# Binding the two stores of an output buffer in order, in a list-scheduled attention and adapter kernel

## Chip, cores and metric

The kernel runs on one core of a Trainium2 chip. The metric is device time in microseconds (us). The kernel before takes 130.53 us (median of 3 runs, 130.23 to 131.1). "The profile" is the record of one execution: its engines are PE (matmul), PEld (weight load), DVE (vector), ACT (scalar), POOL (GpSimd) and SP, which here only issues DMAs. The span of a profile is about 1.8 us shorter than the time of its run. The profiled run of the kernel before took 131.71 us, 1.2 us above the median. A run is called slow when it is over 1.5% above the fastest of its kernel; ratios leave slow runs out.

## The reference

```
q_p, k_p = phi(q), phi(k)            # relu(x) times a cosine and a sine of the position
num = q_p @ (k_p^T v);  den = q_p . sum(k_p) + 1e-6
x   = (num / den), heads side by side          # 4608 rows of 512, float32
logits = x @ w_gate;  the two best of 8 experts, softmax weights w
out = x + sum over the two of  w * (x @ A[e]) @ B[e]
```

Eight batches of q, k and v (28.3 MB with the weights left out) are loaded and 9.4 MB are stored.

## The kernel before

The rows are worked on in 36 groups of 128. One or two groups make a *unit*, which is collected in one output buffer ("osb", a pool of seven). ACT evicts (copies out) the result of a group from PSUM, where PE leaves it, into the buffer (`x_sum`; one of the last is DVE's). Two DMA stores then empty the buffer: y=0 the lower 64 partitions, y=1 the upper 64.

```python
def x_sum(g, eng):                      # eviction of group g
    dx = st[g].pop("dx")
    u, j = unit_of[g]
    if u not in osbs:
        osbs[u] = p_out.tile([NP, 2, DM], FP32, name="osb")    # p_out has bufs=7
    copy(eng, osbs[u][:, j, :], dx)

def store(u, y, eng):                   # half y of unit u
    osb = osbs[u]
    ...
    {"SP": nc.sync, "ACT": nc.scalar, "POOL": nc.gpsimd}[eng].dma_start(
        out=dst[:, x:x + 2 * n - 1:2, :], in_=osb[SP * y:SP * y + SP, 0:n, :])
```

The order of all instructions is made when the kernel is built. Each piece of work is declared as an `op` with its engine, an estimated cost, a priority, what it depends on (`deps`), the buffers that it takes and those that it gives back. A list scheduler (`plan`) goes forward and backward through these declarations and returns an order; the instructions are then emitted in that order. The program itself does not trust the declarations: real semaphores are set from what each instruction truly reads and writes. A wrong declaration can therefore not give a wrong result. It can give a plan in which a real wait is missing.

```python
NB = {..., "osb": 7, ...}               # buffers that the plan counts
for g in range(G):
    ...                                 # cut
    op(("os", g), e, {"ACT": 0.5, "DVE": 0.6}[e], p + 1, lambda g=g, e=e: x_sum(g, e),
       deps=[("dx", g)], take=["osb"] if unit_of[g][1] == 0 else [], give=[bank])
    u, n = unit_of[g]
    if n == len(units[u]) - 1:
        for y in range(2):
            op(("st", u, y), "SP", 0.6, p + 2 + y, lambda u=u, y=y: store(u, y, "SP"),
               deps=[("os", h) for h in units[u]], take=["lane"], lat=1.3)
            op(("out", u, y), "DMA", 0.34 * (n + 1), p + 3 + y, none, deps=[("st", u, y)],
               give=["lane"] + (["osb"] if y else []), lat=0.4)

for n in plan(ops, NB):
    ops[n].fn()
```

("lane" is one of eight DMAs that the plan allows in flight.) The last `give` is the point: the plan hands the buffer back when the store y=1 has landed, and says nothing of y=0.

## Time and profile before

| | kernel before |
|---|---|
| time, median | 130.53 us |
| span of the profile | 129.9 us |
| busy PE / DVE / ACT / POOL | 87.7 / 89.3 / 90.4 / 82.7 us |
| longest wait of an eviction for a store | 11.2 us |
| DMA rate while it is full | about 395 GB/s |

The page of the kernel before cuts the span into 40 slices of 3.25 us; a digit is the busy tenth of a slice (9 is 90% or more), PEclk the granted PE clock in tenths of full speed.

```profile
PE   0007785599989879889978400099998999967400
DVE  0594687845999998899999300058899999984200
ACT  7755079877999978989999300295999656877500
POOL 4035975799999999999985994058999700000000
PEclk9999999856999999999999965557999999999955
DMA  4999999999999999999999999987350164752984
```

About three fifths of the way PE and DVE read 0 for three slices and ACT for two, while DMA stays full and POOL goes on a little longer. The PE clock falls to a half in the same place and recovers only later. The next view puts numbers to it: busy time by stretch (from:to in us, its length, then us busy and instructions of each engine, the granted clock as a share of full speed, DMA share and rate; the DMA share can read a little over 1).

```profile
core 0: us, PE busy (x) PEld busy (x) DVE busy (x) ACT busy (x) POOL busy (x), PEclk, DMA share, GB/s
31.00:72.60 41.60, 36.59 (x732) 29.27 (x741) 38.88 (x121) 38.87 (x96) 39.64 (x74) 0.99 1.05 395
72.60:83.80 11.20, 0.47 (x30) 0.44 (x23) 0.24 (x1) 0.05 (x2) 6.99 (x16) 0.65 1.05 397
83.80:91.80 8.00, 7.14 (x76) 5.65 (x77) 5.16 (x12) 6.41 (x16) 5.32 (x12) 0.64 0.78 219
```

Up to 72.6 us this is a balanced pipeline in which four engines are all over 87% busy. Then there is a hole of 11.2 us. The list of waits (who waited for whom: us in total, times, longest) names its cause:

```profile
PE dx L461 <- ACT osb L197: 12.3, 4, 11.4
DVE wg L430 <- ACT sg L423: 12.0, 2, 11.7
ACT osb L197 <- DMA out_dram<-osb: 11.2, 1, 11.2
...
POOL qp L206 <- PE qTp L335: 6.9, 2, 6.5
```

Read it from the third line. One eviction on ACT waited once, for 11.2 us, for a store. The other lines are followers: ACT executes in order, so PE waits for ACT's eviction, DVE for a sigmoid that stands behind it on ACT, and POOL for PE. The chain that ended last (start, us, what) passes through the same store:

```profile
69.19 0.55 SPq L191
69.74 0.05 issue
69.79 13.90 DMA out_dram<-osb
...
83.79 0.59 ACT osb L197
84.43 0.59 PE dx L461
```

The store that was waited for was put in the queue at 69.79 us, just after the last load (69.19), and landed 13.9 us later. The order in which SP issues DMAs explains why it came so late (place in the queue; buffer numbers kept):

```
20 store osb_703    21 load v    22 load k    23 store osb_703
24 store osb_855    25 store osb_1109     26 load k   27 load v
28 store osb_1227   29 load q    30 load q    31 store osb_1389
32 load k   33 load v   34 store osb_1446     35 load q   (the last load)
36 store osb_855    37 store osb_1109     38 store osb_1553     39 store osb_1227 ...
```

The buffer osb_855 has one half stored at place 24, the other at 36.

The store at place 36 was not slow for its stage, it was issued late. By the landing records of the trace every store that was put in the queue between 39 and 70 us (places 20 to 36) took 10 to 14 us to land. An estimate from the same records agrees: at 69.79 us four loads of 1.18 MB and two stores (0.13 and 0.26 MB) had not landed; with this store that is 5.4 MB, or 13.6 us at 395 GB/s. The other half, at place 24, was issued at 46.61 us and landed at 59.34.

### The profile page before, as it was taken

How to read it: one execution, taken by the hardware profiler on the slowest of the kernel's cores; microseconds unless marked ns; L12 is line 12 of the kernel's file. 1: busy time of each engine (PE TensorE's matmuls, PEld its weight loads, DVE VectorE, ACT ScalarE, POOL GpSimd, SP SyncE). 2: the span in 40 equal slices, each digit the busy share in tenths (PEclk: the TensorE clock that was granted, in tenths of full speed). 3: DMA queues.
4: the chain of work that ended last, by engine and by line, in shares of the span. 5: the costliest groups of instructions: out<-in, count | busy, mean ns of one | idle time of the engine just before them, and what ended most of it. 6: DMA issues, size and time to landing. Idle time of an engine off the chain costs nothing.

```text
span 129.9 us, 4085 instructions
## 1 busy us (share of the span) xinstructions
PE 87.7 (67%) x1580; PEld 69.4 (53%) x1596; DVE 89.3 (69%) x273; ACT 90.4 (70%) x214; POOL 82.7 (64%) x168
## 2 busy tenths in 40 slices
PE   0007785599989879889978400099998999967400
PEld 0007565488667667667757300077786788644100
DVE  0594687845999998899999300058899999984200
ACT  7755079877999978989999300295999656877500
POOL 4035975799999999999985994058999700000000
PEclk9999999856999999999999965557999999999955
DMA  4999999999999999999999999987350164752984
GB/s 120 367 371 358 383 390 395 397 392 382 393 393 387 392 389 402 392 399 405 397 397 395 400 390 405 386 239 194 87 138 32 37 166 124 176 146 87 241 217 107
DMA packets 19379, 38.55 MB, mean 297 GB/s; under 512 B 1696, under 2 KB 2720, under 8 KB 19360
## 3 DMA queue, kind: packets, MB, share of 16 engines
q1 hardware_dynamic: 19360, 38.29, 85.0%
q8 instruction: 12, 0.20, 0.6%
q14 instruction: 7, 0.06, 0.1%
HBM read 28.85 MB, written 9.44 MB: 295 GB/s over the span
## 4 chain that ended last, share of the span: by engine, by line
DVE 25%; DMA 21%; PE 20%; POOL 11%; SPq 8%; issue 5%; ACT 3%; ACTq 0%; POOLq 0%
DMA out_dram<-osb 11%; DMA vf<-in_v_dram 10%; DVE xt L367 9%; POOL qp L206 7%; PE qTp L335 6%; DVE qT L341 5%; SPq L191 4%; PE kvz L299 4%; POOL vb_118 L199 3%; DVE zg L432 3%; DVE xT L199 2%; SPq L486 2%; PE za L397 2%; POOL vb_120 L199 2%; DVE rden L365 2%
## 5 line engine op out<-in xcount | busy, mean ns | idle before, releaser
L206 POOL TENSOR_SCALAR qp<-qf,cos_tab 128x256 bf16<-128x256 f32 x71 | 33.9, 478 | 11.1 <-PE qTp L335 6.9
L204 ACT ACTIVATE kp<-kf,cos_tab 128x256 bf16<-128x256 f32 (+1 forms) x69 | 34.2, 495 | 6.1 <-DMA kf<-in_k_dram 6.1
L206 POOL TENSOR_SCALAR qp<-qf,sin_tab 128x256 bf16<-128x256 f32 x71 | 33.9, 477 | 0.0
L204 ACT ACTIVATE kp<-kf,sin_tab 128x256 bf16<-128x256 f32 (+1 forms) x69 | 33.8, 490 | 0.0
L197 ACT COPY osb<-dx 128x512 f32<-128x512 f32 x31 | 17.9, 579 | 16.5 <-DMA out_dram<-osb 11.2
L341 DVE TENSOR_SCALAR qT<-qTp 128x1024 bf16<-128x1024 bf16 x36 | 24.6, 684 | 5.9 <-PE qTp L335 5.9
L335 PE MATMUL qTp<-ident,qp 128*128 128x128 bf16 x288 | 25.6, 240 | 1.4 <-POOL qp L206 1.2
L367 DVE TENSOR_TENSOR xt<-nd,rden 128x512 bf16<-128x512 f32 x36 | 24.9, 691 | 1.2
L335 PEld LDWEIGHTS <-qp 128*128 128x128 bf16 x288 | 20.3, 108 | 4.4 <-POOL qp L206 1.8
L461 PE MATMUL dx<-xt,ident 128*128 128x512 bf16 x27 | 10.7, 397 | 12.3 <-ACT osb L197 12.3
L299 PEld LDWEIGHTS <-kp 64*128 64x128 bf16 x576 | 12.1, 103 | 12.2 <-ACT kp L204 5.7
L378 PE MATMUL xTp<-ident,xt 128*128 128x128 bf16 x144 | 14.4, 224 | 4.2 <-DVE xt L367 3.4
L397 PE MATMUL za<-AW,xT 128*128 128x136 bf16 x144 | 13.6, 228 | 2.6 <-ACT AW L197 2.3
L378 PEld LDWEIGHTS <-xt 128*128 128x128 bf16 x144 | 9.7, 100 | 10.1 <-DVE xt L367 7.4
L352 PE MATMUL nd<-kvs,qT 128*128 128x65 bf16 x256 | 13.9, 200 | 1.3 <-DVE qT L341 1.0
L352 PEld LDWEIGHTS <-qT 128*128 128x128 bf16 x256 | 11.4, 102 | 3.1 <-DVE qT L341 2.0
L199 DVE COPY xT<-xTp 128x512 bf16<-128x512 bf16 x28 | 11.6, 417 | 1.2 <-PE xTp L378 0.8
L299 PE MATMUL kvz<-vb_116,kp 64*128 64x65 bf16 x216 | 5.5, 208 | 9.6 <-POOL vb_116 L199 9.6
L397 PEld LDWEIGHTS <-xT 128*128 128x128 bf16 x144 | 9.9, 100 | 3.7 <-issue 2.4
L462 PEld LDWEIGHTS <-zT 128*128 128x128 bf16 x36 | 3.6, 99 | 14.1 <-issue 12.6
L430 DVE TENSOR_TENSOR wg<-za,sg 128x24 f32<-128x24 f32 x12 | 2.1, 175 | 12.0 <-ACT sg L423 12.0
L199 POOL CAST vb_116<-vf 128x1152 bf16<-128x1152 f32 x5 | 5.8, 1175 | 6.4 <-DMA vf<-in_v_dram 6.4
(94 smaller groups left out, 110.3 us busy)
## 6 DMA issues: line engine op xcount, KB each, us to landing
kf<-in_k_dram SPq DMA_DIRECT2D x7, 1152.0 KB, 14.7
vf<-in_v_dram SPq DMA_DIRECT2D x7, 1152.0 KB, 15.2
qf<-in_q_dram SPq DMA_DIRECT2D x7, 1152.0 KB, 14.3
out_dram<-osb SPq DMA_DIRECT2D x28, 256.0 KB, 4.9
out_dram<-osb SPq DMA_DIRECT2D x16, 128.0 KB, 2.4
kf<-in_k_dram SPq DMA_DIRECT2D x2, 576.0 KB, 4.2
vf<-in_v_dram SPq DMA_DIRECT2D x2, 576.0 KB, 7.0
qf<-in_q_dram SPq DMA_DIRECT2D x1, 640.0 KB, 9.7
```

What stands on the lines that cost most here:

```text
L197: nc.scalar.copy(dst, src)
L199: {"DVE": nc.vector, "POOL": nc.gpsimd}[eng].tensor_copy(dst, src)
L204: nc.scalar.activation(dst, src, AF.Relu, bias=0.0, scale=scale)
L206: {"DVE": nc.vector, "POOL": nc.gpsimd}[eng].tensor_scalar(out=dst, in0=src, scalar1=scale, scalar2=0.0 if relu else 1.0, op0=ALU.mult, op ...
L299: nc.tensor.matmul(out=kvz_t[b][:, e, i * W:(i + 1) * W], lhsT=kps[b, x][ps, i], rhs=vb[ps, i, x, :], start=(x == 0), stop=(x == X - 1))
L335: nc.tensor.transpose(out=qTp[:, i, :, y, :], in_=qp[:, i], identity=ident)
L341: nc.vector.tensor_scalar_max(qT, qTp.rearrange("f i e y p -> f (i e) (y p)"), 0.0)
L352: nc.tensor.matmul(out=nd[:, gg, cs], lhsT=qT[:, h, :], rhs=kv_sb[b0][:, h, :], start=True, stop=True)
L367: nc.vector.tensor_tensor(out=xt, in0=nd_v[:, :, :, 0:D], in1=rden.rearrange("p (g j) -> p g j", g=2).to_broadcast([NP, 2, 4, D]), op=ALU. ...
L378: nc.tensor.transpose(out=xTp[:, c, :], in_=xt[:, c * 128:(c + 1) * 128], identity=ident)
L397: nc.tensor.matmul(out=za[:, i, :], lhsT=xT[:, c, :], rhs=AW[:, c, :], start=(c == 0), stop=(c == DCH - 1))
L461: nc.tensor.matmul(out=dx, lhsT=ident, rhs=xt, start=True, stop=False)
```

## The change

Its intent: the store y=1, with which the plan gives the buffer back, is made to depend on the store y=0, so that it can't be planned ahead of it.

```diff
             for y in range(2):
                 op(("st", u, y), "SP", 0.6, p + 2 + y, lambda u=u, y=y: store(u, y, "SP"),
-                   deps=[("os", h) for h in units[u]], take=["lane"], lat=1.3)
+                   deps=[("st", u, 0)] if y else [("os", h) for h in units[u]],
+                   take=["lane"], lat=1.3)
```

No instruction is added or removed. The plan is made anew, so the order changes on every engine.

## The prediction

> **What bounds the kernel now.** The page of the kernel before (span 129.9 us) shows four engines at 64 to 70% and DMA at nine tenths in nearly every slice up to 85 us. The averages hide three stages. A table of busy time by stretch gives:
>
> - 31 to 72.6 us: a balanced pipeline. DVE is busy 38.9 of 41.6 us, ACT 38.9, POOL 39.6, PE 36.6, for 18 groups: 2.3 us each.
> - 72.6 to 83.8 us: a hole. PE is busy 0.5 us, DVE 0.2, ACT 0.05; only POOL runs ahead (7.0), and DMA stays full. The list of waits has the cause in one line: the ACT eviction into an output buffer (osb) waited 11.2 us, once, for the DMA out_dram<-osb. PE's wait on that eviction (11.4), DVE's on ACT's sigmoid (11.7) and POOL's (6.5) follow. The chain that ended last agrees: 13.9 us of DMA out_dram<-osb from 69.79, then the eviction at 83.79.
> - After that: 14 groups, at first at a granted clock of 0.60; the last stores end at 129.9.
>
> **Why the hole is there.** Two stores empty a buffer. The plan gives it back with the second (y=1), but nothing ordered the two. For the unit whose buffer is reused at the hole, and others, y=1 was queued early and y=0 twelve places later, behind the last loads; the real dependence waits for both. The issue order shows it: one half is at place 24 of the queue, the other at 36. The Trainium skill, "DMA: Bandwidth & Descriptors", section "Queues, rings and completion order", says that each engine consumes descriptors in ring order; the trace agrees: a 256 KB store, 4.9 us to landing in the median, took 13.9 behind the last loads.
>
> **What the change does.** No instruction is added or removed; the plan is made anew. In the changed order the two stores of a unit mostly stand next to each other. The three units of the hole's kind have theirs at 24/25, 27/29 and 30/31, ahead of the last loads. The critical reuses left are of the units stored at 35/36 and 39/40, five and seven groups after the hole's group, about 12 and 16 us later. I estimate that 40 lands near 85 and is wanted near 89 us. So I expect no long stall, at most 1 to 2 us.
>
> **The sum.** Removed: 11.2 us, all on the critical path, and the slow restart (6.3 us of PE work at clock 0.60), some 1.2 us. Given back: what POOL and the loads did in the hole must now overlap with the pipeline, and ten stores instead of seven precede the last load (0.8 MB, 2 us at 395 GB/s). POOL's 24 us of work left at 72.6 can end near 97: no new bound, but little slack. I estimate 1.2 us. 130.5 - 11.2 - 1.2 + 1.2 = 119.3.
>
> **Prediction:** 119.3 us, 80% range 116.5 to 122.5. Faster by over 2%: 0.96; within 2%: 0.03; slower: 0.01.
>
> **What would show it.** No eviction waits over 3 us for a store; no empty DVE slice and no clock dip around 75 to 90 us; DVE busy about 89 us in a span near 118.7; the stage before 72 us within 1 us; POOL ending near 97. If ACT still waits on a store, its size tells how much only moved.
>
> **What would make it wrong.** The new order may delay a load (the fifth batch's v, or the last q), so that POOL waits for DMA; the unit stored at 39/40 may be wanted before it lands; or the new plan may be worse in its first third.

## The result

The changed kernel takes 118.04 us (median of 4 runs, 117.16 to 118.39); the kernel before, run beside it, 130.81 us. The ratio is 0.9015 (95% interval 0.8949 to 0.9081). Ratios here are the mean time of one kernel's fast runs over that of the other's fast runs of the same rounds, so they are not quite the ratios of the medians quoted. A later repeat of the changed kernel gave 117.51 us and 0.8964 (0.8920 to 0.9008). The profiled run was the fastest of the first four (span 115.4 us; the other three 116.1 to 116.6), so the profile flatters it by about 1 us, and the two spans (129.9 and 115.4) overstate the gain.

Slices of the page of the changed kernel, each 2.9 us:

```profile
PE   0006498469878897979999679999899898985200
DVE  0595469937799999989999997999999989953200
ACT  7874209898999998499999999999998377777300
POOL 4003995779999999999999689999999991000000
PEclk9999999976999999999999999999999999999955
DMA  3999999999999999999999999999999865855884
```

The zeros and the dip of the clock in the third quarter are gone. DMA now stays full until about four fifths of the span. Busy time by stretch, for the same stretches as before:

```profile
31.00:72.60 41.60, 36.35 (x747) 29.52 (x755) 39.18 (x124) 39.17 (x97) 39.99 (x78) 1.00 1.05 394
72.60:83.80 11.20, 10.66 (x214) 8.53 (x215) 10.59 (x30) 11.20 (x29) 11.20 (x23) 1.00 1.05 394
83.80:91.80 8.00, 7.16 (x138) 5.96 (x138) 7.76 (x23) 6.20 (x16) 8.00 (x16) 1.00 0.96 328
```

The first stretch has not changed. The second, which held 0.24 us of DVE work, now holds 10.59. In the third PE is busy as long as before (7.16 and 7.14 us), but gets through 138 instructions instead of 76: a PE that is busy at half clock for most of the stretch gets less done (the mix of instructions differs too). The view of the output buffer in the changed kernel, the part about what its engine waited for:

```profile
its engine sat idle before it (us, times) until:
  PE dx L462: 4.8, 4
  PE dx_2982 L462: 0.7, 1
  PE nd L352: 0.5, 1
  PE zTp L444: 0.5, 1
  PE dx_3030 L462: 0.3, 1
...
DMA to landing us min/median/max: 2.3/4.3/14.9
```

No eviction waits for a store any more. The last line deserves a look: some store still took 14.9 us to land, longer than the 13.9 us of before. Stores are as slow as they were behind the loads; this one was issued at 44.4 us. What has gone is somebody waiting for one.

### The profile page after: what moved, and what is told of

It is laid out like the page before. It is cut to its first block, busy times and chain, and to the rows that moved or that the text cites. A ratio compares the mean times of both kernels' runs of the same rounds, so it can differ in the third digit from the quotient of the medians.

```text
span 115.4 us, 4086 instructions
## 1 busy us (share of the span) xinstructions
PE 83.7 (73%) x1580; PEld 67.0 (58%) x1596; DVE 88.7 (77%) x273; ACT 90.2 (78%) x214; POOL 82.4 (71%) x168
## 4 chain that ended last, share of the span: by engine, by line
DVE 55%; PE 21%; DMA 7%; issue 3%; ACT 3%; SPq 2%; POOL 1%; ACTq 0%; POOLq 0%
DVE xt L367 18%; DVE qT L341 16%; DMA qf<-in_q_dram 7%; PE qTp L335 6%; DVE xT L199 6%; PE za L397 4%; PE kvz L299 4%; DVE rden L365 4%; DVE zg L432 3%; PE nd L352 2%; SPq L191 2%; PE xTp L378 1%; DVE u L412 1%; DVE zT L199 1%; DVE lm L410 1%
## 5 line engine op out<-in xcount | busy, mean ns | idle before, releaser
L335 PE MATMUL qTp<-ident,qp 128*128 128x128 bf16 x288 | 23.5, 228 | 1.8 <-POOL qp L206 0.8
L335 PEld LDWEIGHTS <-qp 128*128 128x128 bf16 x288 | 19.3, 103 | 4.9 <-issue 1.6
L299 PEld LDWEIGHTS <-kp 64*128 64x128 bf16 x576 | 11.5, 101 | 11.6 <-issue 5.1
L352 PE MATMUL nd<-kvs,qT 128*128 128x65 bf16 x256 | 13.7, 197 | 1.8 <-DVE qT L341 1.6
L199 POOL CAST vb_116<-vf 128x1152 bf16<-128x1152 f32 x5 | 5.7, 1147 | 6.1 <-DMA vf<-in_v_dram 6.1
L462 PE MATMUL dx<-Ball,zT 128*128 128x512 bf16 x22 | 8.3, 379 | 0.4 <-DVE zT L199 0.2
L199 POOL CAST vb_118<-vf 128x1152 bf16<-128x1152 f32 x6 | 6.7, 1149 | 2.0 <-DMA vf<-in_v_dram 2.0
```

What stands on the lines that cost most here:

```text
L199: {"DVE": nc.vector, "POOL": nc.gpsimd}[eng].tensor_copy(dst, src)
L299: nc.tensor.matmul(out=kvz_t[b][:, e, i * W:(i + 1) * W], lhsT=kps[b, x][ps, i], rhs=vb[ps, i, x, :], start=(x == 0), stop=(x == X - 1))
L335: nc.tensor.transpose(out=qTp[:, i, :, y, :], in_=qp[:, i], identity=ident)
L352: nc.tensor.matmul(out=nd[:, gg, cs], lhsT=qT[:, h, :], rhs=kv_sb[b0][:, h, :], start=True, stop=True)
```

## The experiments

Two theories were set against each other. Theory A: the hole was the wait of one buffer reuse for one late store, and that is all that the change removed. Rival B: the gain comes from the new plan, which orders every engine differently. A third, C, was that the loads would limit the kernel anyhow, so that the wait would come back elsewhere.

### More real buffers, with no instruction moved

The plan still counts seven buffers, so the order of all engines is exactly that of the kernel before (compared instruction by instruction in the built programs). Only the pool has more buffers, so that the late-stored one is wanted later.

```diff
-    p_out = ctx.enter_context(tc.tile_pool(name="p_out", bufs=7))
+    p_out = ctx.enter_context(tc.tile_pool(name="p_out", bufs=8))     # and 9, 10, 11
```

> The kernel before, with eight real output buffers instead of seven while the plan still counts seven; every engine's order is that of the kernel before. Theory A (the hole is the wait of one reuse for the late y=0 store at place 36): the buffer that is stored at 24/36 is now wanted by the unit of group 17 instead of 15, two groups or 4.6 us later at 2.3 us per group, so the wait of ACT on a store falls from 11.2 to about 6.6 us and the time from 130.8 to about 126.2 (124.5 to 127.5). Rival B (the gain of the change comes from the plan made anew, not from the reuse): same as before within 1%.

> As the run with eight, with nine real buffers. Theory A: wanted by the unit of group 18, three groups or 6.9 us later: a wait of about 4.3 us, 123.9 us (122 to 125.5). Rival B: same as before within 1%.

> As the run with eight, with eleven real buffers: the buffer stored at 24/36 is wanted by the unit of group 22, seven groups or 16 us later, after the store has landed. Theory A: no eviction waits for a store, 118 to 119.5 us, as the changed kernel within 1%, although no instruction has moved. Rival B: same as before. Rival C (the loads were the limit behind the hole, so that removing it only moves the wait to a load): 122 us or more with new waits of POOL or ACT on loads.

> As the runs with eight, nine and eleven real buffers, now ten. The late-stored buffer is then wanted by the unit of group 20, whose eviction started at 82.5 us in the run with eleven; its store landed at 83.2 to 84.2 us in the runs of before, eight and nine. Theory A: a wait of 1 to 2 us and, as PE isn't idle long enough to lose its clock, 119 to 120.5 us. If nine buffers failed to gain on eight for a reason other than the time at which the store lands, ten will stay over 122 us.

| real buffers | time, us (median) | ratio to before (95%) | start of the waiting eviction | its wait | span |
|---|---|---|---|---|---|
| 7 (before) | 130.53 | 1 | 83.79 | 11.15 | 129.9 |
| 8 | 126.63 | 0.9674 (0.9589 to 0.9758) | 83.26 | 6.82 | 124.9 |
| 9 | 126.76 | 0.9651 (0.9600 to 0.9702) | 84.19 | 6.88 | 125.1 |
| 10 | 120.95 | 0.9225 (0.9173 to 0.9276) | 84.04 | 3.09 | 119.5 |
| 11 | 118.22 | 0.8995 (0.8938 to 0.9052) | none waits | 0 | 116.8 |

(Eight, nine and eleven ran beside the same runs of the kernel before, at 131.37 us; ten beside others, at 130.87.) The waiting eviction in the timelines of ACT, for eight, nine and ten buffers (start, us, what, and in brackets the idle time before it and what ended it):

```profile
83.26 0.58 ACT L197 COPY osb<-dx 128x512 f32<-128x512 f32 x1 [6.82 <-DMA out_dram<-osb]
```

```profile
84.19 0.58 ACT L197 COPY osb<-dx 128x512 f32<-128x512 f32 x1 [6.88 <-DMA out_dram<-osb]
```

```profile
84.04 0.58 ACT L197 COPY osb<-dx 128x512 f32<-128x512 f32 x1 [3.09 <-DMA out_dram<-osb]
```

And the same view of the output buffer as above, with eleven:

```profile
its engine sat idle before it (us, times) until:
  PE dx L462: 6.0, 9
  PE qTp L335: 0.9, 2
```

In all four runs with a wait it ends at 83.3 to 84.2 us (with nine buffers one more eviction waits, for 0.3 us, at 117.3): the store lands when it lands, behind the loads, and only the time at which somebody asks for it moves. With eleven buffers no one asks before it is there, and the time is that of the changed kernel, although no instruction has moved. That rejects B as the main cause, and C: the loads did not give the time back.

Nine buffers were a miss: 123.9 us was expected, 126.76 measured. The estimate had put the next eviction 2.3 us later. In the profile with nine buffers ACT had been about 1.2 us ahead since the first third and asked only 0.9 us later (77.3 instead of 76.4), and the store landed 0.9 us later too. In the profiled run the place of the loss can be seen. The 8 us after the wait, with eight and with nine (columns as above):

```profile
83.26:91.26 8.00, 7.31 (x116) 5.71 (x117) 4.22 (x9) 7.36 (x18) 8.00 (x16) 0.72 0.87 260
84.19:92.19 8.00, 7.15 (x103) 5.82 (x103) 3.72 (x13) 5.93 (x14) 8.00 (x16) 0.58 0.85 246
```

With nine the clock stayed at half until 90.9 us, against 87.8 with eight, and ACT idled 2.07 us for PE just before its eviction at 90.52. Whether the other runs with nine, which were no faster either, lost it in the same way is not on record. Ten buffers also waited longer than expected (3.1 us instead of 1 to 2), again because the eviction came early, at 80.95 instead of 82.5; and PE did lose its clock, against what was expected (see the last section).

The pair of before and eleven buffers, which differ in nothing but this wait, also gives the full price of the hole. The normalisations of DVE (start of the n-th reciprocal in each profile, us):

| n-th | before | eleven buffers | changed kernel |
|---|---|---|---|
| 14 | 54.82 | 54.64 | 50.15 |
| 22 | 70.38 | 70.21 | 68.71 |
| 23 (first after the hole) | 87.74 | 75.29 | 73.86 |
| 27 | 98.70 | 85.57 | 82.61 |
| 36 (last) | 115.18 | 102.06 | 100.61 |

In the rows before the hole the two run together to 0.2 us. At the first group after it they are 12.45 us apart, from the 27th on 13.1, as are the spans (129.9 - 116.8) and the medians of these rounds (131.37 - 118.22). So the wait of 11.15 us cost 13.1: about 2 us more, lost on the restart. The slow clock goes with this, 0.64 on average for 8 us, but no run took the clock away alone, so its share is argued, not shown. Ten buffers are a hint: their clock was at half for 3.4 us only (13.7 in the kernel before), and their wait of 3.09 us cost no more than itself (2.7 by the spans of ten and eleven).

### Only the stores moved

The plan of the kernel before, with seven buffers; each y=0 store that it had placed behind its y=1 is emitted just before it.

```diff
-    for n in plan(ops, NB):
+    order = plan(ops, NB)
+    at = {n: i for i, n in enumerate(order)}
+    for u in range(len(units)):
+        i, j = at["st", u, 0], at["st", u, 1]
+        if i > j:
+            order.remove(("st", u, 0))
+            order.insert(order.index(("st", u, 1)), ("st", u, 0))
+    for n in order:
         ops[n].fn()
```

> The plan of the kernel before with seven buffers; only each y=0 store that it had put behind its y=1 is moved up to just before it. All engines but the DMA-issuing one keep their order. Theory A: no wait over 3 us of an eviction for a store, 118 to 120 us: the place of the store in the queue is all that mattered, and the new plan adds less than 1.5 us. Rival B: at least half the gain missing, over 124 us.

Measured: 119.59 us, ratio 0.9105 (0.9047 to 0.9162). No eviction waits for a store; the view of the output buffer, as above:

```profile
its engine sat idle before it (us, times) until:
  PE dx L462: 5.6, 8
  PE qTp L335: 2.8, 2
```

Theory A holds here too: the place of seven stores in the queue makes some nine tenths of the gain. The 1.4 us that are missing against eleven buffers have a likely cause that the profile shows. The gaps in which POOL waited for a load from 60 us on, first in this run, then with eleven buffers:

```profile
67.86 2.23 POOL L199 CAST vb<-vf 128x1152 bf16<-128x1152 f32 x2 [2.41 <-DMA vf<-in_v_dram]
72.25 0.48 POOL L206 TENSOR_SCALAR qp<-qf,cos_tab 128x256 bf16<-128x256 f32 x1 [2.15 <-DMA qf<-in_q_dram]
```

```profile
65.88 2.23 POOL L199 CAST vb<-vf 128x1152 bf16<-128x1152 f32 x2 [0.41 <-DMA vf<-in_v_dram]
69.64 0.48 POOL L206 TENSOR_SCALAR qp<-qf,cos_tab 128x256 bf16<-128x256 f32 x1 [1.52 <-DMA qf<-in_q_dram]
```

The stores that moved up push the loads back, and POOL waits 2.6 us longer for them in these two places. This is the give-back that the prediction feared. (This profile also has a dip of the clock to half, from 75.3 to 78.7 us, that eleven buffers have not; how the 1.4 us divide was not tested.) The new plan of the changed kernel, which knows of the earlier stores, avoids it: after 60 us its POOL waits for no load, and it comes out level with eleven buffers.

### A true release without a bound order

The stores stay unordered, but the plan gives the buffer back only when both have landed.

```diff
                 op(("out", u, y), "DMA", 0.34 * (n + 1), p + 3 + y, none, deps=[("st", u, y)],
-                   give=["lane"] + (["osb"] if y else []), lat=0.4)
+                   give=["lane"], lat=0.4)
+            op(("rel", u), "REL", 0.0, p + 4, none, deps=[("out", u, 0), ("out", u, 1)],
+               give=["osb"])
```

> Kernel before, the two stores left unordered, but the plan gives the buffer back only when both have landed (a release step that depends on both). If the fault was the plan's wrong belief about the release and not the missing order as such, this does as well as the changed kernel: 117 to 119.5 us, no eviction waiting over 2 us for a store. If binding the order matters by itself, over 121 us.

Measured: 117.34 us (fast runs 116.91 to 117.46; one of four, the profiled one, was slow at 118.74), ratio 0.8947 (0.8895 to 0.8999). So the order need not be bound: the fault was the plan's belief about the release. Once the belief is true, the scheduler itself plans the two stores of most units in neighbouring places; in the built programs SP's order of DMAs is the very same as in the changed kernel. A build that bound them the other way round (y=0 after y=1, release still with y=1) was not run: its plan came out, on every engine but SP, as that of the kernel before. On SP only the 14 units that had y=0 first had their two stores swapped; the late ones stayed late.

### Can the end be made shorter?

The changed kernel's last eviction starts at 107.58 us, but the last store is issued at 112.01. Its timelines of ACT and of SP:

```profile
107.58 0.58 ACT L197 COPY osb<-dx_3030 128x512 f32<-128x512 f32 x1 [0.28 <-PE dx_3030 L462]
```

```profile
112.01 0.59 SPq L486 DMA_DIRECT2D out_dram<-osb  x1
```

Ten small stores queue up at 0.6 us each on one issuer. The changed kernel was run with some of them issued by another engine:

```diff
-   op(("st", u, y), "SP", 0.6, p + 2 + y, lambda u=u, y=y: store(u, y, "SP"),
+   e = "ACT" if g == G - 1 else "SP"                                  # tail_act, planned so
+   op(("st", u, y), e, 0.6, p + 2 + y, lambda u=u, y=y, e=e: store(u, y, e),
# tail_pool: planned for SP, emitted on POOL:  e="POOL" if y and g >= G - SINGLE else "SP"
# tail_act2: emitted on ACT, and moved to the end of the order
```

> Changed kernel; the last unit's two stores are issued by ACT instead of the SP queue, all else in the same order. In the changed kernel's profile the last eviction ended at 108.2 us but its second store was issued only at 112.0, as SP takes 0.6 us for each of the last ten. Two issues fewer at the end: 1.2 us off the changed kernel's 118.0, so 116.8 (116.0 to 117.5). If the drain is set by the transfers and not by their issue, no gain.

> Changed kernel; the second store of each of the last five units is issued by the idle POOL instead of SP, all else in the same order. Five issues fewer on SP, some of which hid behind waits for evictions: 1.5 to 3 us off, 115 to 116.5 us, unless POOL's own issue takes longer than SP's 0.6 us; then a part of it, or a loss.

> The changed kernel again, unaltered, so that the next two have it beside them in the same rounds: 117.2 to 118.6 us, 0.895 to 0.908 of the kernel before.

> The last unit's two stores on ACT again, but now last in program order, so that no SP store waits for the landing of one of ACT's, as one did for 2.8 us in the first try. The last issue should end near 110 us of the profile instead of 112.6. If the drain of issues is what ends the kernel: 1.5 to 2.5 us below the changed kernel of these rounds. If the landing of the last transfers sets it: under 0.7 us.

> The plan with the true release (117.3 us, fast runs 116.9 to 117.5) together with the last unit's stores on ACT, last in program order: if both gains hold, 114.5 to 116.2 us, below both the kernel before and the changed kernel; if the 0.7 us of the true release was chance among plans, equal to the run before this one.

> The plan with the true release together with the second stores of the last five units on the idle POOL, which no store of SP waited for in the earlier run. If the 0.7 us of the true release and the 0.8 us of POOL's issues are both real and add, 115.5 to 116.7 us, a ratio to the kernel before of 0.882 to 0.892, below the changed kernel's 0.896; if one of them was chance, 0.892 to 0.900.

| run | time, us | ratio to before (95%) |
|---|---|---|
| changed kernel, again | 117.51 | 0.8964 (0.8920 to 0.9008) |
| last unit's stores on ACT | 119.91 (two fast runs: 118.0, 118.8) | none: four of six runs slow |
| the same, last in the order | 118.23 (four fast runs: 117.67 to 118.70) | 0.8995 (0.8951 to 0.9038) |
| the same, with the true release | 118.40 (four fast runs: 117.51 to 118.80) | 0.9001 (0.8956 to 0.9046) |
| second stores of five units on POOL | 116.73 | 0.8926 (0.8877 to 0.8974) |
| the same, with the true release | 117.14 | 0.8926 (0.8884 to 0.8968) |

ACT brought nothing: the fast runs lie at or above the repeat of the changed kernel. All three runs with ACT missed the gain that was hoped for. The list of SP's waits in the second try shows where it went:

```profile
SPq L486 <- DMA out_dram<-osb: 2.1, 2, 1.9
```

(This profile fell in a slow run.) The listing of the built program shows that the DMAs of both issuers take turns at eight completion semaphores, and that the two semaphores missing from SP's turn, those of ACT's pair, are then waited on by SP's two stores of the third unit from the end. The trace agrees: ACT's two stores, issued from 110.48 us, landed at 112.89 and 113.70; SP's next two were issued at 112.95 and 113.72. Moving the pair to the end of the order did not change this. The Trainium skill, "DMA: Bandwidth & Descriptors", section "Issuing engines are not separate DMA queues", says that issuing from several engines "will only save the time on the sequencer it takes to initiate the DMA"; here a wait behind a shared semaphore ate that saving. With POOL, whose five DMAs have semaphores of their own in the built program, SP had no such wait in the middle. The two runs on POOL and the true release have medians below the changed kernel's, by 0.2 to 0.8 us, but all their intervals overlap with its own and they were not in its rounds. None is shown to beat it; the ratio 0.8926 of the two together is what was expected if one of the small gains was chance.

## Why the prediction was right, point by point

- *The hole is one wait for a late store, 11.2 us, all on the critical path.* Right: eleven buffers, with nothing else changed, give 0.8995, the change 0.9015 and 0.8964.
- *No long stall is left.* Right: no eviction waits for a store, and no clock dip. The unit stored at places 39/40 was feared for; nobody waited: place 40 landed at 86.45 us (forecast near 85), and its buffer was next written at 89.29 (near 89).
- *The restart costs 1.2 us.* Too small. Before and eleven buffers differ by 13.1 us of span for 11.15 us of wait: 2.0 us, net of anything given back.
- *1.2 us are given back to the loads and POOL.* Not seen in the result. A loss of that kind (1.4 us) appears when the stores are moved and nothing is planned anew, but the new plan is built around the earlier stores. (The ten stores are 0.66 MB more than the seven, not 0.8, as those of a one-group unit have half the size.) These two terms were set to cancel. The change measured 130.81 - 118.04 = 12.8 us, 1.6 more than the wait itself, and that is where 118.04 parts from the predicted 119.3.
- *The stage before 72 us unchanged within 1 us.* Its busy times are, but not its progress: the changed kernel was 4.7 us ahead at the 14th normalisation and 1.7 at the 22nd. Against eleven buffers, which keep the old order, it was 4.5, 1.5 and in the end 1.45 us ahead; but this profile is of its fastest run, and by the medians the two are level (118.04 and 118.22, of different rounds). So no gain of the new order over the old one is shown.
- *POOL ends near 97, DVE busy about 89.* POOL ended at 96, DVE was busy 88.7 us.

## What to carry to other kernels

When a plan is made by a model of the program, compare its beliefs with the real dependences: a buffer is free when its *last* reader is done, and a release tied to one of two unordered readers invites the scheduler to postpone the other. In the profile such a fault looks like one single long wait of a producer for a buffer, with the issue of the DMA just behind a batch of loads. Adding real buffers while the plan still counts the old number is a quick test of it that moves no instruction.

## What the Trainium skill lacked or had wrong

- "TensorE: Matmul & The Clock Gate", Part 1, says that the clock falls to half after about 3.4 us of idle time, recovers after about 3.4 us of sustained work (about 4 in its example), and that the window is free-running. The runs agree on the half (0.50), but the recovery took up to 2 us more: from PE's first matmul to full clock 3.9 us with eight buffers (83.9 to 87.8), 5.1 in the kernel before (84.4 to 89.5), 6.1 with nine (84.8 to 90.9). In the clock records of these traces and of ten buffers the slow stretches about the wait last 6.83, 13.65, 10.24 and 3.41 us, all whole multiples of 3.41 us. That fits the free-running window, and would explain a recovery that takes between one window and two, but no run tests it. The page does not say that the fall can come after work has resumed. With ten buffers PE was idle for only 2.9 us, at full clock (84.3 to 87.2), and fell to half at 88.3 us, while busy. The stretches of that run, columns as above:

```profile
84.30:87.20 2.90, 0.00 (x0) 0.00 (x0) 0.79 (x3) 2.90 (x9) 2.90 (x5) 1.00 0.83 259
87.20:89.00 1.80, 1.72 (x27) 1.61 (x29) 1.73 (x6) 1.80 (x5) 1.80 (x5) 0.80 0.92 232
89.00:91.00 2.00, 1.86 (x15) 1.57 (x15) 1.83 (x4) 1.49 (x4) 2.00 (x6) 0.50 0.86 257
```

- "DMA: Bandwidth & Descriptors", section "Latency and other measured facts", speaks of a fixed cost of about 2 us for a DMA; the shortest landing of a store here was 2.3 us. Missing is what a full queue does to it: a 256 KB store issued behind the last loads landed after 13.9 us, against a median of 4.9 us for the 28 stores of that size in the kernel before, and all stores issued in the full stage there took 10 to 14 us. In this kernel that is the number to plan buffers with.
- The same page, section "Issuing engines are not separate DMA queues", does not warn that DMAs of two issuers may share completion semaphores, so that one issuer waits for the other's transfer (1.9 us here). The sharing was laid out in the built program of this kernel.
